# Second layer's weight operands made during the first layer through four buffers and stored to DRAM

## The chip, the cores and the metric

One core of a Trainium2 chip. The time is device microseconds of one execution of the whole kernel; where several runs are named, it is their median. TensorE multiplies, ACT (ScalarE), DVE (VectorE) and POOL (GpSimd) do everything elementwise, SP (SyncE) issues nearly all DMAs. Each engine works through its own queue in order.

## The reference

Float32 all through. Attention in chunks of 32 queries over a window of keys plus 8 memory keys, for 4 x 8 heads of 768 x 64; its output, laid out as x of 3072 tokens x 512, goes through two feed-forward layers:

```python
# per chunk of 32 queries: mem_k, mem_v and 16 positions to the left, 8 to the right
a = softmax(q_c @ [mem_k, k_ctx].T / 8);  attn_c = a @ [mem_v, v_ctx]
x = attn, heads side by side                     # 3072 x 512
h = x @ moe_w_in;  x = (h * cos(h)) @ moe_w_out  # layer 1, d_ff 2048
h = max(max(x @ w1, x @ w2), x @ w3)             # layer 2, d_ff 768
out = h @ moe2_w_out
```

## The kernel before, in words

**Split operands.** TensorE's operands have the type fp32r, so each float32 operand is kept as two tiles, high part and remainder, and each product is three matmuls (`PASSES`). The weights arrive as 64-bit words; making an operand out of a raw tile `[128, 512, 2]` takes: the load (`w_load`, L163), the exponent part (`w_top`, ACT or POOL, L174), the mantissa merged into it (`w_bits`, DVE, L185), and the split, a copy on ACT and a subtraction on DVE or POOL (`w_split` L199 for layer 1 and w_out of layer 2, `q_split` L500 for w1 to w3).

**Layer 1.** The tokens are 8 blocks j = 0 to 7 of 384, d_ff is 16 chunks f of 128. A slot is one (j, f): `p1` (L384) makes h with 12 matmuls, `chain` (L399) makes g = h cos h on ACT, DVE, ACT, DVE, ACT, POOL (L421 to L431), `p2` (L435) multiplies g with w_out two slots later, 12 more matmuls into four accumulators. There are 128 slots; the order is blocks 0 to 5, then blocks 6 and 7 in halves, and `turn`, slot 104, is the first of block 7. Between p1 and p2 a slot can hold a piece of the attention of the next block (tables `FIRST` to `STEADY`: S scores, E exponentials, N normalizing, T transposes, V values). Block results go to DRAM (`x2d`).

**Layer 2.** Four pairs p of blocks. For each pair nine quads q, each a pair of 128-column chunks of one of w1, w2, w3, as seven products of 6 matmuls in place of eight (`PRODUCTS`, sums and differences of weights and of x), so 42 matmuls of 384 columns a quad and 378 a pair. The results are copied out of PSUM (`snap`, L705, ACT), added (L708) and maximized. Then 108 matmuls with w_out of layer 2 (L780). A quad reads four operand tiles from DRAM (`wd`), three of 512 KB and one of 256 KB, fetched three quads ahead (`q_fetch`, L515).

**Preparation.** `wd` must be made first, out of w1 to w3: eight steps for each of nine quads (`q_steps`, L522: tops, bits, four POOL sums, four splits, then `q_store`, L509, which stores four tiles), and two steps for each of six chunks of w_out (`o_steps`, L555), which stay on chip. `Prep` (L563) loads and steps through this from slot `turn` on, in the 24 last slots of layer 1 up to three steps a slot (`fill`, L879), and goes on inside the quads of pair 0 (L981 to L984). It uses the 32 buffers of pool `wp`, which hold all weights of layer 1; a buffer comes free when block 7 has used its weight. `live` counts them.

**Order.** A scheduler orders each engine's instructions when the kernel is built: by program order, but an instruction whose inputs are expected earlier may go ahead. `keep` puts an instruction behind the one traced just before it on its engine. Instructions of the preparation are kept on ACT, DVE and POOL; loads and stores on SP are not.

Of the kernel before, what the change touches and what calls it, by code (L numbers as in the profile page):

```python
# [9 lines left out]
F32 = mybir.dt.float32  # L10
# [60 lines left out]

NW, NTOP = 32, 2
RATE = 2
STEPS = 3

# [5 lines left out]
def attn_moe_kernel(ctx, tc, qT, kT, vw, w_in, w_out, w3, w2o, out):  # L83
# [22 lines left out]
    ps_acc = ctx.enter_context(tc.tile_pool(name="ps_acc", bufs=1, space=PSUM))  # L106
    ps_h = ctx.enter_context(tc.tile_pool(name="ps_h", bufs=2, space=PSUM))
    ps_a = ctx.enter_context(tc.tile_pool(name="ps_a", bufs=2, space=PSUM))
    att_cm = tc.tile_pool(name="att", bufs=2)
    t2 = att_cm.__enter__()  # L110
    tmp = {}
# [51 lines left out]
    def w_load(key):  # L163

        kind, i = key
        src = SRC[kind][i] if kind != "b" else w3[i[0], i[1]]
        t = wp.tile([128, 512, 2], I32, tag="w", name="raw")
        live[0] += 1
        SP.dma_start(out=t.rearrange("p c t -> p (c t)").bitcast(U16)[:, :2047], in_=src.bitcast(U16)[:, 1:])
        wst[key] = t  # L170

# [13 lines left out]
    def w_bits(key):  # L185

        z = o = wst[key][:, :, 0]
        if key[0] == "out" and key[1] < PLAIN:
            i, odd = divmod(key[1], 2)
            if not odd:  # L190
                plain[i] = (wp if i < PLAIN // 2 - 1 else tmp["pool"]).tile([128, 2, 512], I32, tag="w", name="wt")
                live[0] += i < PLAIN // 2 - 1
            o = plain[i][:, odd, :]
            live[0] -= 1
            DST[key[0]][key[1]] = o.bitcast(F32)
        keep(DVE.scalar_tensor_tensor(o, z, 13, top[key], op0=ALU.logical_shift_right, op1=ALU.bitwise_or))  # L196
        wst[key] = o.bitcast(F32)
# [258 lines left out]
    hB, xs, x2, wq, post = {}, {}, {}, {}, {}  # L456
    bank = [0]
    wd = [[dp.tile([128, 1024 if i < 3 else 512], F32, name=f"wd{q}_{i}") for i in range(4)] for q in range(NQ)]

    def w_tile(shape, name, dtype=F32R):  # L460
        live[0] += 1
        assert live[0] <= NW
        return wp.tile(shape, dtype, tag="w", name=name)
# [36 lines left out]
    def q_split(q, i, eng):  # L500
        ev, od = q_parts(q)
        src = (ev[0], ev[1], od[0], od[1][:, :256])[i]
        n = 512 if i < 3 else 256
        w = w_tile([128, 2, n], "wq")
        keep(ACT.activation(out=w[:, 0, :], in_=src, func=AF.Copy))
        keep(eng.tensor_tensor(w[:, 1, :], src, w[:, 0, :].bitcast(F32), op=ALU.subtract))
        wq["new", q, i] = w

    def q_store(q):  # L509
        for i in range(4):  # L510
            w = wq.pop(("new", q, i))
            SP.dma_start(out=wd[q][i], in_=w.rearrange("p a c -> p (a c)").bitcast(F32))
            live[0] -= 1

    def q_fetch(p, q):  # L515
        for i in range(4):
# [5 lines left out]
    def q_steps(q):  # L522

        a, b = q_pair(q)

        def bits(k):
            raw = wst[k]
            w_bits(k)
            wst[k] = raw
        L, R = slice(0, 256), slice(256, 512)  # L530

        def s_31():
            ev, od = q_parts(q)
            q_sub(POOL, od[0][:, L], ev[0][:, L], ev[1][:, L])
            q_sub(POOL, ev[1][:, L], ev[1][:, L], ev[1][:, R], ALU.add)

        def s_2():
            ev, od = q_parts(q)
            q_split(q, 0, DVE)
            q_sub(POOL, od[0][:, R], ev[1][:, L], ev[0][:, L])  # L540

        def s_4():
            ev, od = q_parts(q)
            q_sub(POOL, od[1][:, L], ev[0][:, R], od[0][:, R])
            q_split(q, 1, DVE)

        def end():
            q_split(q, 3, POOL)
            live[0] -= 2
            wst.pop(a), wst.pop(b), qs.pop(q)  # L550
            q_store(q)
        return [lambda: w_top(a, ACT), lambda: (w_top(b, ACT), bits(a)), lambda: bits(b), s_31, s_2, s_4,
                lambda: q_split(q, 2, DVE), end]

    def o_steps(f):  # L555
        key = ("bo", f)

        def go():
            w_top(key, ACT)
            w_bits(key)  # L560
        return [go, lambda: w_split(key, DVE)]

    class Prep:  # L563


        def __init__(self):
            self.nl = self.n = 0
            self.loads = [("q", q) for q in range(NQ)] + [("o", f) for f in range(FB)]
            self.steps = [(i, fn) for i, (kind, n) in enumerate(self.loads)
                          for fn in (q_steps(n) if kind == "q" else o_steps(n))]  # L570

        def load(self):
            while self.nl < len(self.loads):
                ahead = self.nl - (self.steps[self.n][0] if self.n < len(self.steps) else self.nl)
                if ahead >= (2 if self.loads[self.nl][0] == "q" else 3):
                    return
                kind, n = self.loads[self.nl]
                if live[0] + (8 if kind == "q" else 3) > NW:
                    return
                if kind == "q":  # L580
                    q_load(n)
                else:
                    w_load(("bo", n))
                self.nl += 1

        def go(self, n=1):
            for _ in range(n):
                if self.n < len(self.steps) and self.steps[self.n][0] < self.nl - (self.nl < len(self.loads)):
                    if self.steps[self.n][0] < NQ and live[0] + 1 > NW:
                        return  # L590
                    self.steps[self.n][1]()
                    self.n += 1

        def made(self):
            return self.steps[self.n][0] if self.n < len(self.steps) else len(self.loads)


    def x_load(p, which=(0, 1)):
# [243 lines left out]
                w_split(("out", self.ns), POOL if self.ns % 2 else DVE)  # L842
                self.ns += 1

    tmp_open("wt", 1)
    dec = Decode(keysA, lambda n: POOL if n < 6 or n % 2 else ACT, lambda n: POOL if n % 2 else DVE)
    for c in LOADS.split():
        if c[0] == "q":
# [16 lines left out]
    def slot(s):  # L865
# [13 lines left out]
        def fill(where):  # L879
            if s < 2:  # L880
                if where == "z":
                    dec.split_in(ready)
                    dec.bits()
                    dec.load()
                return
            if s >= turn:
                if where == "z":
                    prep.load()
                    for fn in early.get(s - total, ()):
                        fn()  # L890
                    if s < total - 6:
                        prep.go(1)
                elif where in ("a0", "d0"):
                    prep.go(1)
                return
            if where == "a0":
                dec.split_in(ready)
            elif where == "a1":
                dec.split_out(parts)
            elif where == "d0":  # L900
                dec.bits(1)
            elif where == "z":
                dec.bits()
                dec.exp(dec.nb + 2)
                dec.load()
# [31 lines left out]
                a_load_v(d + 2)  # L937
        do2()

    prep = Prep()  # L940
    early = {}
    ops0 = {}

# [1 line left out]
        x_sum(0)  # L945
        ops0.update(x_ops(0))

    early[-9] = [lambda: x_load(0)]
    early[-7] = [begin0, lambda: ops0["b11"]()]
    early[-6] = [lambda: ops0["t1"]()]  # L950
    early[-5] = [lambda: ops0["t2"]()]
    early[-4] = [lambda: ops0["t4"]()]
    early[-3] = [lambda: ops0["b22"](), lambda: ops0["t3"](), lambda: q_fetch(0, 0)]
    early[-2] = [lambda: q_fetch(0, 1)]
    early[-1] = [lambda: ops0["rest"]()]
    for s in range(total):
        if s == turn:
            tmp_close()
            att_cm.__exit__(None, None, None)
            tmp_open("ph2", 2)  # L960
            done[0] = True
            prep.load()
        slot(s)
        if s < PINNED:
            hold()
    hold(False)
    rest = [slots[i] for i in range(n2[0], total)]
    for p in range(NP):
        for q in range(NQ):
            for n in quad(p, q):  # L970
                if p == 0 and q == 0 and n < 3:
                    while len(rest) > (2, 1, 0)[n]:
                        p2(*rest.pop(0))
                if n == 0:
                    if p == 0 and q == 0:
                        q_fetch(0, 2)
                    nxt = divmod(p * NQ + q + AHEAD, NQ)
                    if nxt[0] < NP and (nxt[0] == p or parts[2 * p + 2] == 1 or nxt[1] == 0):
                        assert p or nxt[0] or prep.made() > nxt[1], (q, prep.made())
                        q_fetch(*nxt)  # L980
                if p == 0:  # L981
                    if n % 2 == 0:
                        prep.load()
                    prep.go(STEPS if n == 6 else 1)  # L984
                if q == NQ - 2 and n == 0 and p + 1 < NP:
                    x_load(p + 1, (0,))
                if q == NQ - 1 and n == 0 and p + 1 < NP:
                    x_load(p + 1, (1,))
# [82 lines left out]
```

## Time and profile before

| | us |
|---|---|
| median of 3 runs | 1059.85 (1059.73 to 1060.57) |
| profiled execution | 1060.66 |
| its span | 1058.9 |
| TensorE busy, weight loads busy | 1007.4, 959.0 |
| DVE, ACT, POOL busy | 572.5, 501.4, 405.4 |

The mean granted TensorE clock is 0.982 of full speed. The busy time of TensorE is modelled from pipelined matmuls, so 95% busy is not 95% of its peak; idle time of an engine that others don't wait for costs nothing. In the rows below PE is TensorE, PEld its weight loads, L705 is line 705 of the kernel, and "x <- y" in the name of an instruction is what it writes and reads.

### The profile page before, as it was taken

How to read it: one execution, taken by the hardware profiler on the slowest of the kernel's cores; microseconds unless marked ns; L12 is line 12 of the kernel's file. 1: busy time of each engine (PE TensorE's matmuls, PEld its weight loads, DVE VectorE, ACT ScalarE, POOL GpSimd, SP SyncE). 2: the span in 40 equal slices, each digit the busy share in tenths (PEclk: the TensorE clock that was granted, in tenths of full speed). 3: DMA queues.
4: the chain of work that ended last, by engine and by line, in shares of the span. 5: the costliest groups of instructions: out<-in, count | busy, mean ns of one | idle time of the engine just before them, and what ended most of it. 6: DMA issues, size and time to landing. Idle time of an engine off the chain costs nothing.

```text
span 1058.9 us, 17399 instructions
## 1 busy us (share of the span) xinstructions
PE 1007.4 (95%) x6732; PEld 959.0 (91%) x6733; DVE 572.5 (54%) x1002; ACT 501.4 (47%) x930; POOL 405.4 (38%) x370
## 2 busy tenths in 40 slices
PE   8799999999999999999999997676999999999998
PEld 5679999999999999999999997666989989999997
DVE  7876566554554545454444676565544464464451
ACT  5578555545555554545544565444333333333331
POOL 4575453333333333333223555462423342433330
PEclk9999999999999999999999998987999999999999
DMA  9951111111111211110112676999339718746601
GB/s 293 361 235 46 53 61 61 67 39 39 67 38 38 68 38 41 65 38 29 48 55 74 244 263 218 397 413 380 132 139 348 257 52 345 231 181 229 247 1 60
DMA packets 55906, 158.67 MB, mean 150 GB/s; under 512 B 6288, under 2 KB 11664, under 8 KB 55824
## 3 DMA queue, kind: packets, MB, share of 16 engines
q1 hardware_dynamic: 55680, 157.43, 41.7%
q8 instruction: 53, 0.87, 0.3%
q14 instruction: 29, 0.24, 0.1%
q10 hardware_dynamic: 144, 0.13, 0.0%
HBM read 126.86 MB, written 30.67 MB: 149 GB/s over the span
## 4 chain that ended last, share of the span: by engine, by line
PE 80%; DMA 10%; DVE 3%; ACT 2%; issue 2%; POOL 2%; SPq 1%; POOLq 0%; ACTq 0%; DVEq 0%
PE h L382 22%; PE hb L684 21%; PE acc L382 21%; PE hb L780 9%; DMA wq<-wd 3%; PE s L242 3%; DMA raw<-in_w_out_dram 2%; PE s L296 2%; PE s L280 2%; DMA k<-in_kT_dram 1%; DMA raw<-in_w_in_dram 1%; DMA raw<-in_w_dram 1%; DMA wd<-wq 1%; DMA raw<-in_w2o_dram 1%; DVE raw L196 0%
## 5 line engine op out<-in xcount | busy, mean ns | idle before, releaser
L382 PE MATMUL h<-x,w 128*128 128x384 f32 x1536 | 291.4, 337 | 5.2 <-DVE g L413 3.8
L382 PEld LDWEIGHTS h<-x,w 128*128 128x128 f32 x1536 | 266.8, 188 | 9.9 <-DVE g L413 4.7
L382 PE MATMUL acc<-g,w 128*128 128x384 f32 x1440 | 273.7, 338 | 1.8 <-POOL g L431 0.7
L382 PEld LDWEIGHTS acc<-g,w 128*128 128x128 f32 x1440 | 252.1, 189 | 3.5 <-DVE x L450 1.2
L431 POOL TENSOR_TENSOR g<-ki,g 128x384 fp32r<-128x384 f32 x112 | 115.0, 1027 | 265.9 <-ACT g L430 213.3
L684 PE MATMUL hb<-x,wq 128*128 128x384 f32 x864 | 157.3, 336 | 7.1 <-DMA wq<-wd 7.1
L684 PEld LDWEIGHTS hb<-x,wq 128*128 128x128 f32 x864 | 151.6, 189 | 7.6 <-DVE ki L424 7.4
L684 PE MATMUL hb<-xo,wq 128*128 128x384 f32 x648 | 125.8, 349 | 26.3 <-ACT a L705 26.3
L684 PEld LDWEIGHTS hb<-xo,wq 128*128 128x128 f32 x648 | 119.5, 198 | 27.5 <-ACT a L705 27.5
L423 DVE SCALAR_TENSOR_TENSOR ki<-h,ki 128x384 f32<-128x384 f32 x112 | 62.1, 555 | 121.2 <-ACT ki L421 121.2
L426 ACT ACTIVATE ki<-ki,pio 128x384 f32<-128x384 f32 x112 | 68.9, 616 | 90.8 <-DVE ki L424 90.8
L780 PE MATMUL hb<-w,g 128*128 128x512 f32 x432 | 98.7, 389 | 0.0
L428 DVE TENSOR_TENSOR ki<-h,ki 128x384 f32<-128x384 f32 x112 | 62.4, 557 | 64.2 <-ACT ki L426 64.0
L780 PEld LDWEIGHTS hb<-w,g 128*128 128x128 f32 x432 | 81.0, 188 | 16.7
L421 ACT ACTIVATE ki<-h 128x384 int32<-128x384 f32 x112 | 54.5, 487 | 71.8 <-PE h L382 69.9
L708 POOL TENSOR_TENSOR p<-p,p 128x384 f32<-128x384 f32 x36 | 36.8, 1023 | 133.4 <-ACT p L705 133.4
L430 ACT ACTIVATE g<-ki 128x384 fp32r<-128x384 f32 x112 | 58.6, 524 | 60.2 <-DVE ki L428 59.8
L708 DVE TENSOR_TENSOR a<-a,hb 128x384 f32<-128x384 f32 x36 | 19.9, 553 | 79.9 <-PE hb L684 79.9
L424 DVE TENSOR_SCALAR ki<-ki 128x384 f32<-128x384 f32 x112 | 53.5, 477 | 2.7
L708 POOL TENSOR_TENSOR p<-p,u 128x384 f32<-128x384 f32 x36 | 37.3, 1036 | 41.4 <-ACT u L705 39.9
L196 DVE SCALAR_TENSOR_TENSOR raw<-raw,top 128x512 int32<-128x512 int32 x48 | 41.1, 862 | 20.9 <-ACT top L179 20.7
L272 POOL TENSOR_TENSOR sm<-sm,rs 128x768 f32<-128x768 f32 x21 | 31.2, 1491 | 54.8 <-DVE rs L271 48.9
(115 smaller groups left out, 1108.8 us busy)
## 6 DMA issues: line engine op xcount, KB each, us to landing
wq<-wd SPq DMA_DIRECT2D x108, 512.0 KB, 7.1
wd<-wq SPq DMA_DIRECT2D x27, 512.0 KB, 3.8
v<-in_vw_dram SPq DMA_DIRECT2D x24, 384.0 KB, 4.5
wq<-wd SPq DMA_DIRECT2D x36, 256.0 KB, 7.7
raw<-in_w_dram SPq DMA_DIRECT2D x18, 511.8 KB, 6.0
raw<-in_w_in_dram SPq DMA_DIRECT2D x16, 511.8 KB, 10.2
raw<-in_w_out_dram SPq DMA_DIRECT2D x16, 511.8 KB, 10.2
k<-in_kT_dram SPq DMA_DIRECT2D x24, 320.0 KB, 4.4
```

The source lines that it names most:

```text
L196: keep(DVE.scalar_tensor_tensor(o, z, 13, top[key], op0=ALU.logical_shift_right, op1=ALU.bitwise_or))
L382: PE.matmul(o, lhsT=w[a][:, sl], rhs=x[b], start=first and n == 0, stop=last and n == 2)
L421: ACT.activation(out=ki, in_=h, func=AF.Copy, scale=INV2PI, bias=0.25)
L423: DVE.scalar_tensor_tensor(c, h, INV2PI, ki, op0=ALU.mult, op1=ALU.subtract)
L424: DVE.tensor_scalar(c, c, -0.75, 0.25, op0=ALU.max, op1=ALU.min)
L426: ACT.activation(out=c, in_=c, func=AF.Sin, scale=2 * math.pi, bias=pio2)
L428: DVE.tensor_tensor(c, h, c, op=ALU.mult)
L430: ACT.activation(out=g[:, 0, :], in_=c, func=AF.Copy)
L431: POOL.tensor_tensor(g[:, 1, :], c, g[:, 0, :].bitcast(F32), op=ALU.subtract)
L684: keep(PE.matmul(o, lhsT=w[:, a, 256 * half + 128 * c:256 * half + 128 * c + 128], rhs=x[c][:, b, :], start=first and n == 0, stop=n == 5, ...
L708: keep(eng.tensor_tensor(o, a, b, op=op))
L780: keep(PE.matmul(o, lhsT=g[:, i, 128 * m:128 * m + 128], rhs=w[k], start=(f == 0 and n == 0), stop=(f == FB - 1 and n == 2)))
```

## The change

All operands of layer 2 are made by slot 101, from slot 31 on: at the end of each slot's `chain` the list `prep` is brought up to int((s - 30) x 1.4) of its 99 steps. The list has one step more than before for each load (nine for a quad, three for a chunk of w_out), so a load comes one step before its first use. Raw tiles and operands of the preparation share four buffers of 4 KB a partition in a new pool `pre`; each operand is stored as soon as it is split, and that frees its buffer. The operands of w_out are stored too (`wod`), and fetched in quads 2 to 4 of pair 0, two a quad (`o_fetch`). Nothing is prepared from slot 102 on. `x_load(0)` moves one slot earlier, the fetches of quads 0, 1 and 2 move to slots total-9, total-3 and total-2. The one buffer of pool `wt` is taken from `pre` instead, and the scratch of the DMA rings shrinks to 1024 bytes.

```diff
-STEPS = 3
+PREP0, PREPS = 30, 1.4
...
+    pre = ctx.enter_context(tc.tile_pool(name="pre", bufs=4))
...
     def w_load(key):
...
-        t = wp.tile([128, 512, 2], I32, tag="w", name="raw")
-        live[0] += 1
+        if kind[0] == "b":
+            t = pre.tile([128, 512, 2], I32, tag="p", name="raw")
+        else:
+            t = wp.tile([128, 512, 2], I32, tag="w", name="raw")
+            live[0] += 1
...
     def q_split(q, i, eng):
...
-        w = w_tile([128, 2, n], "wq")
+        store(src, n, eng, wd[q][i])
+
+    def store(src, n, eng, dst):
+        w = pre.tile([128, 2, n], F32R, tag="p", name="wq")
         keep(ACT.activation(out=w[:, 0, :], in_=src, func=AF.Copy))
         keep(eng.tensor_tensor(w[:, 1, :], src, w[:, 0, :].bitcast(F32), op=ALU.subtract))
-        wq["new", q, i] = w
-
-    def q_store(q):
-        for i in range(4):
-            w = wq.pop(("new", q, i))
-            SP.dma_start(out=wd[q][i], in_=w.rearrange("p a c -> p (a c)").bitcast(F32))
-            live[0] -= 1
+        SP.dma_start(out=dst, in_=w.rearrange("p a c -> p (a c)").bitcast(F32))
...
     def q_steps(q):
...
-        return [lambda: w_top(a, ACT), lambda: (w_top(b, ACT), bits(a)), lambda: bits(b), s_31, s_2, s_4,
+        return [lambda: q_load(q), lambda: w_top(a, ACT), lambda: (w_top(b, ACT), bits(a)), lambda: bits(b), s_31, s_2, s_4,
                 lambda: q_split(q, 2, DVE), end]
...
     def o_steps(f):
...
-        return [go, lambda: w_split(key, DVE)]
-
-    class Prep:
...
+        return [lambda: w_load(key), go, lambda: store(wst.pop(key), 512, DVE, wod[f])]
+
+    prep = [fn for q in range(NQ) for fn in q_steps(q)] + [fn for f in range(FB) for fn in o_steps(f)]
+    prep_n = [0]
+
+    def prep_go(upto):
+        while prep_n[0] < min(upto, len(prep)):
+            prep[prep_n[0]]()
+            prep_n[0] += 1
+
+    def o_fetch(f):
+        w = w_tile([128, 2, 512], "wo")
+        SP.dma_start(out=w.rearrange("p a c -> p (a c)").bitcast(F32), in_=wod[f])
+        wB_out[f] = (w[:, 0, :], w[:, 1, :])
...
         def fill(where):
...
             if s >= turn:
                 if where == "z":
-                    prep.load()
                     for fn in early.get(s - total, ()):
                         fn()
-                    if s < total - 6:
-                        prep.go(1)
-                elif where in ("a0", "d0"):
-                    prep.go(1)
                 return
+            if where == "z":
+                prep_go(int((s - PREP0) * PREPS))
...
-    early[-9] = [lambda: x_load(0)]
+    early[-10] = [lambda: x_load(0)]
...
-    early[-3] = [lambda: ops0["b22"](), lambda: ops0["t3"](), lambda: q_fetch(0, 0)]
-    early[-2] = [lambda: q_fetch(0, 1)]
+    early[-9] = [lambda: q_fetch(0, 0)]
+    early[-3] = [lambda: ops0["b22"](), lambda: ops0["t3"](), lambda: q_fetch(0, 1)]
+    early[-2] = [lambda: q_fetch(0, 2)]
...
                 if n == 0:
-                    if p == 0 and q == 0:
-                        q_fetch(0, 2)
+                    if p == 0 and 1 < q < 5:
+                        o_fetch(2 * q - 4)
+                        o_fetch(2 * q - 3)
...
-                if p == 0:
-                    if n % 2 == 0:
-                        prep.load()
-                    prep.go(STEPS if n == 6 else 1)
...
-    nc = bacc.Bacc("TRN2", target_bir_lowering=False, num_devices=1)
+    nc = bacc.Bacc("TRN2", target_bir_lowering=False, num_devices=1, dynamic_dma_scratch_size=1024)
```

## Rows read from the trace of the kernel before

**Rows 1.** The page's 40 slices, in tenths: TensorE busy, granted clock:
```profile
PE   8799999999999999999999997676999999999998
...
PEclk9999999999999999999999998987999999999999
```

**Rows 2.** Stretches: length; busy PE, PEld, DVE, ACT, POOL; clock, DMA share, GB/s:
```profile
108.00:150.00 42.00, 40.12 (x296) 38.18 (x295) 26.46 (x47) 24.80 (x42) 21.12 (x17) 1.00 0.18 62
...
230.00:530.00 300.00, 300.00 (x2319) 294.31 (x2318) 151.18 (x288) 155.19 (x254) 95.79 (x85) 1.00 0.14 46
...
574.00:626.00 52.00, 52.00 (x301) 51.68 (x299) 34.06 (x55) 31.34 (x61) 30.09 (x31) 1.00 0.63 226
...
644.50:760.60 116.10, 82.75 (x416) 81.50 (x416) 63.94 (x98) 50.14 (x97) 50.28 (x49) 0.84 0.90 344
```

**Rows 3.** Chain of waits: start, length, what; pair 1's products:
```profile
785.12 65.54 PE hb L684 x378
```

**Rows 4.** Waits of TensorE, 600 to 780 us: total, times, longest:
```profile
PE hb L684 <- ACT a L705: 26.3, 4, 9.4
PE hb L684 <- DMA wq<-wd: 7.1, 1, 7.1
PE acc L382 <- ACT x L448: 0.5, 1, 0.5
PE acc L382 <- DVE x L450: 0.4, 1, 0.4
```

**Rows 5.** Timeline of TensorE: start, length, what, idle before it:
```profile
721.62 4.92 PE L684 MATMUL hb<-xo,wq 128*128 128x384 f32 x18 [9.43 <-ACT a L705]
```

**Rows 6.** Waits of ACT for loads, 640 to 765 us:
```profile
ACT top L179 <- DMA raw<-in_w_dram: 12.5, 4, 9.7
...
ACT top L179 <- DMA raw<-in_w2o_dram: 9.7, 2, 7.3
```

**Rows 7.** Groups, 560 to 760.6 us: count, busy us, mean ns, idle before:
```profile
L486 POOL TENSOR_TENSOR raw<-raw 128x256 f32<-128x256 f32 x36 | 33.4, 928 | 20.1 <-DVE raw L196 18.4
...
L506 DVE TENSOR_TENSOR wq<-raw,wq 128x512 fp32r<-128x512 f32 x27 | 26.1, 969 | 19.9 <-ACT wq L505 19.8
...
L179 ACT ACTIVATE top<-raw 128x512 f16<-128x512 bf16 x24 | 18.4, 782 | 22.2 <-DMA raw<-in_w_dram 12.5 <-DMA raw<-in_w2o_dram 9.7
...
L505 ACT ACTIVATE wq<-raw 128x512 fp32r<-128x512 f32 x27 | 17.7, 667 | 16.0 <-POOL raw L486 9.5 <-DMA wd<-wq 4.9 <-DMA wq<-wd 1.6
...
L196 DVE SCALAR_TENSOR_TENSOR raw<-raw,top 128x512 int32<-128x512 int32 x24 | 17.4, 733 | 20.7 <-ACT top L179 20.7
```

**Rows 8.** DMA of 785 to 850 us, beside pair 1's products:
```profile
DMA packets 5910, 18.43 MB, mean 283 GB/s; under 512 B 656, under 2 KB 656, under 8 KB 5904
```

**Rows 9.** Timeline, a plain slot of block 3:
```profile
294.87 1.01 POOL L431 TENSOR_TENSOR g<-ki,g 128x384 fp32r<-128x384 f32 x1 [3.57 <-PE acc L382]
...
300.02 2.24 PE L382 MATMUL acc<-g,w 128*128 128x384 f32 x12
```

**Rows 10.** Timeline, a slot with an exponential; its table loads, 190 to 530 us:
```profile
311.12 0.56 DVE L428 TENSOR_TENSOR ki<-h,ki 128x384 f32<-128x384 f32 x1 [0.57 <-ACT ki L426]
...
314.11 2.24 PE L382 MATMUL h<-x,w 128*128 128x384 f32 x12
...
L264 ACT ACT_TABLE_LOAD x13 | 16.7, 1283 | 0.2
```

**Rows 11.** Timeline of block 1, a slot with an exponential and a split:
```profile
121.98 0.62 PE L382 MATMUL h<-x,w 128*128 128x384 f32 x2 [1.10 <-DVE ki L428]
```

**Rows 12.** Timeline: DVE's clamp alone, and beside POOL's L486:
```profile
301.40 0.36 DVE L424 TENSOR_SCALAR ki<-ki 128x384 f32<-128x384 f32 x1
...
593.62 4.22 POOL L486 TENSOR_TENSOR raw<-raw 128x256 f32<-128x256 f32 x4
...
594.15 1.02 DVE L424 TENSOR_SCALAR ki<-ki 128x384 f32<-128x384 f32 x1
```

**Rows 13.** DMA issues, 544 to 620 us: count, KB each, us to landing:
```profile
raw<-in_w_dram SPq DMA_DIRECT2D x10, 511.8 KB, 4.5
```

More of the change, by code (lines that the diff above doesn't have):

```diff
@@ L190, in w_bits @@
             if not odd:
-                plain[i] = (wp if i < PLAIN // 2 - 1 else tmp["pool"]).tile([128, 2, 512], I32, tag="w", name="wt")
+                plain[i] = (wp if i < PLAIN // 2 - 1 else pre).tile([128, 2, 512], I32, tag="w" if i < PLAIN // 2 - 1 else "p", name="wt")
                 live[0] += i < PLAIN // 2 - 1
@@ L458, in attn_moe_kernel @@
     wd = [[dp.tile([128, 1024 if i < 3 else 512], F32, name=f"wd{q}_{i}") for i in range(4)] for q in range(NQ)]
+    wod = [dp.tile([128, 1024], F32, name=f"wod{f}") for f in range(FB)]
     def w_tile(shape, name, dtype=F32R):
@@ L548, in end @@
             q_split(q, 3, POOL)
-            live[0] -= 2
             wst.pop(a), wst.pop(b), qs.pop(q)
-            q_store(q)
-        return [lambda: w_top(a, ACT), lambda: (w_top(b, ACT), bits(a)), lambda: bits(b), s_31, s_2, s_4,
+        return [lambda: q_load(q), lambda: w_top(a, ACT), lambda: (w_top(b, ACT), bits(a)), lambda: bits(b), s_31, s_2, s_4,
                 lambda: q_split(q, 2, DVE), end]
@@ L560, in go @@
             w_bits(key)
-        return [go, lambda: w_split(key, DVE)]
-    class Prep:
[L566 to L595, printed above, removed]
+        return [lambda: w_load(key), go, lambda: store(wst.pop(key), 512, DVE, wod[f])]
[9 more added lines that the diff above has]
+        wB_out[f] = (w[:, 0, :], w[:, 1, :])
     def x_load(p, which=(0, 1)):
@@ L843, in split_out @@
                 self.ns += 1
-    tmp_open("wt", 1)
     dec = Decode(keysA, lambda n: POOL if n < 6 or n % 2 else ACT, lambda n: POOL if n % 2 else DVE)
@@ L938, in slot @@
         do2()
-    prep = Prep()
     early = {}
@@ L957, in attn_moe_kernel @@
         if s == turn:
-            tmp_close()
             att_cm.__exit__(None, None, None)
@@ L974, in attn_moe_kernel @@
                 if n == 0:
-                    if p == 0 and q == 0:
-                        q_fetch(0, 2)
+                    if p == 0 and 1 < q < 5:
+                        o_fetch(2 * q - 4)
+                        o_fetch(2 * q - 3)
                     nxt = divmod(p * NQ + q + AHEAD, NQ)
                     if nxt[0] < NP and (nxt[0] == p or parts[2 * p + 2] == 1 or nxt[1] == 0):
-                        assert p or nxt[0] or prep.made() > nxt[1], (q, prep.made())
                         q_fetch(*nxt)
-                if p == 0:
-                    if n % 2 == 0:
-                        prep.load()
-                    prep.go(STEPS if n == 6 else 1)
                 if q == NQ - 2 and n == 0 and p + 1 < NP:
```

## The prediction

> **What bounds the kernel now.** I read the page's 40 slices first [rows 1]. The row PE stands at 9 nearly from end to end, except in slices 25 to 28 (26.5 us each), where it falls to 7676; PEclk dips there too. So TensorE bounds the kernel everywhere but in one hole. The table by stretch says the same in numbers [rows 2]: in 230 to 530 us, steady blocks of layer 1, TensorE is busy 300.00 of 300.00 us while DVE (151.18), ACT (155.19) and POOL (95.79) are half or two thirds idle; in 644.5 to 760.6, where pair 0 of layer 2 runs with the last three steps of layer 1, it is busy only 82.75 of 116.1 us, at a granted clock of 0.84 of its higher level (2.4 GHz).
>
> What pair 0 should cost stands in the chain of waits [rows 3]: pair 1 runs the same 378 matmuls of 384 columns without a gap in 65.54 us, 173.4 ns each. Between 644.5 and 760.6 TensorE runs 36 matmuls of layer 1 and those 378 of pair 0: 414 x 0.1734 = 71.8 us. It takes 116.1, so 44.3 us are lost. TensorE's own waits say where [rows 4]: four of 26.3 us in sum and one of 7.1, together 33.4; the rest, 82.75 - 71.8 = 10.95 us, goes to matmuls that run at a lower granted clock after a wait, as the 18 that take 4.92 us after the longest wait [rows 5], where 18 x 0.1734 are 3.1.
>
> Who holds TensorE there: the first wait ends with the fetch wq<-wd, the other four with "ACT a L705", the copy that empties a PSUM bank. That copy is short; it stands in ACT's order behind instructions of the preparation which wait for a DMA. The waits of 640 to 765 us name them [rows 6]: top (L179) for the raw weights of w1 to w3, 12.5 us with 9.7 the longest, and for those of w_out, 9.7 with 7.3. So the hole is preparation that waits for a whole DMA, with TensorE's evictions queued behind it.
>
> **The change, part by part.** *Removed from 540 to 760 us:* all loads, splits and stores of the preparation. The five large groups [rows 7] are ACT 18.4 + 17.7 = 36.1 us, DVE 26.1 + 17.4 = 43.5 and POOL 33.4; the smaller copies and subtractions of the same steps I estimate from them at 8, 4 and 10 more (nine half-size copies, nine POOL subtractions, and six splits of w_out at the 0.67 and 0.97 us of the large ones): 44, 48 and 43. With it go the waits of [rows 6]. The fetch for (0, 0) is issued in slot total-9 instead of total-3, behind no store of that time, so its 7.1 us go. What is late next? In pair 0 the engines then do what they do in pair 1, and there TensorE has no gap [rows 3]. The DMA traffic is pair 1's 18.43 MB [rows 8] plus the six fetches of wod, 3.1 MB: 21.5 MB in 65.5 us, 329 GB/s, below the 344 GB/s of the stretch in question [rows 2]. Quads 2 to 4, with a double load, need 1.84 + 1.05 = 2.9 MB in 7.28 us, 397 GB/s, but each fetch is issued three quads (21.8 us) ahead. I cost this at nothing; if that cover went, a wait like the 7.1 us would come back. Gain here: 44.3 us. Two short waits near 626 us, 0.5 and 0.4 us [rows 4], where accumulator copies stood behind preparation on ACT and DVE, go as well: 0.9 us.
>
> *Moved into slots 31 to 101* (by the position of the blocks some 190 to 530 us): 99 steps at 1.4 a slot. The 44, 48 and 43 us lie beside 340 us of TensorE at work, 13 to 14% more for each engine: DVE 50 to 64%, ACT 52 to 65%, POOL 32 to 45%. No engine becomes the bound. What can hurt is delay on the path from p1 through chain to p2. In a plain slot [rows 9] a g is done at 294.87 + 1.01 = 295.88 us, and the p2 that reads it, two steps on, starts at 300.02: 4.1 us to spare. A slot gets one or two steps, which put about two instructions of 0.67 to 0.97 us ahead of a link on an engine: it fits. In a slot with an exponential ACT has two table loads ahead of the sine; h is freed by DVE L428 only at 311.12 + 0.56 = 311.68, and the p1 that needs the buffer starts at 314.11 [rows 10]: 2.4 us to spare. Such slots are 13 in 190 to 530 us (13 table loads of L264 [rows 10]).
>
> The trace has two stretches like it. Lower bound, 574 to 626 us: up to three steps a slot, DVE busy 66%, POOL 58%, and TensorE 52.00 of 52.00 [rows 2]; but no attention there, and more buffers for h. Upper bound, 108 to 150 us: attention plus seven weight splits, and TensorE 40.12 of 42.00 [rows 2]; at that rate 340 us would lose 1.88 / 42 x 340 = 15.2 us. The larger of its two waits, 1.10 us [rows 11], falls in a slot with an exponential and an added split. At 1.4 steps a slot 0.4 of the slots get two steps; I let those of the 13 lose as much: 13 x 0.4 x 1.10 = 5.7 us, nearer to the lower end, and keep 0 and 15.2 for the range.
>
> The port that DVE and POOL share is the other way in. Beside a POOL subtraction the clamp of the chain (DVE L424) takes 1.02 us instead of 0.36 [rows 12]. POOL gets 45 more instructions; within 4.1 us of room one of them costs nothing, and if the clamp waits out one of 0.93 us [rows 7] in those 13 x 0.4 slots, that is 4.8 us on top. The Trainium skill, "SBUF — State Buffer", section "SBUF: two separate sides", says that the pair of ports is an exclusive lock and that the loser blocks for the whole instruction. By that rule the 4.8 us are lost and the time is 1025.2 us; the trace agrees on the lock, 1.02 against 0.36, and shows no wait of TensorE from it in 574 to 626.
>
> *Waits added.* Four buffers hold two raw tiles and two operands, so the third operand's ACT copy waits for the first one's store, and the next load for the last subtraction; behind these copies on ACT stand the next link of chain, then p2. ACT's order is written by expected times, so what is left is their error. In 544 to 620 us a raw load lands in 4.5 us [rows 13], against 4.1 us of room: nothing, or a few tenths. On SP the loads for attention, a block ahead of use, and the x2d stores stand behind these DMAs: nothing. The wt buffer moves to another pool, and the smaller DMA scratch serves no queue used here (SP and ACT issue all): nothing.
>
> *Sum* against the profiled execution (1060.66 us, span 1058.9): 1060.66 - 44.3 - 0.9 + 5.7 = 1021.2. It lies 0.81 above the median of the runs, 1059.85, so the forecast is 1020.4 us.
>
> **The rivals.** (a) *The moved work costs more in blocks 2 to 6.* For it: the rate of 108 to 150 us. Against it: 574 to 626 us without a loss. At the upper bound, 15.2 instead of 5.7: 1059.85 - 45.2 + 15.2 = 1029.9 us. With the port's share on the forecast: 1020.4 + 4.8 = 1025.2.
> (b) *Pair 0 stays hungry.* The fetches bunch with wod in quads 2 to 4, and waits like the 7.1 and one of 9.4 us [rows 4] stay, with slow clock in proportion (10.95 / 33.4 = 0.33 us per us of wait): 16.5 x 1.33 = 21.9, time 1020.4 + 21.9 = 1042.3. For it: 397 GB/s wanted there. Against: pair 1 without a gap.
> (c) *Slower: four buffers tie ACT to the DMA.* Each load is issued one step before its first use, no longer up to two pairs ahead, and ACT stands at its head through the landing, with chain behind it. There are 15 such places (nine pairs, six chunks of w_out). If each waits like the longest of [rows 6], 9.7 us, less the 4.1 of room, that is 15 x 5.6 = 84 us, time 1059.85 - 45.2 + 84 = 1098.7. It decides from 45.2 / 15 = 3.0 us net a place, 7.1 us at ACT's head. For it: exactly such waits made the hole. Against: they came with the DMA 90% busy; in 230 to 530 it is 14% [rows 2], and in 574 to 626, at 63%, loads of about that time landed in 4.5 us.
> (d) *It doesn't do what it says*: every operand is fetched from DRAM either way, and nothing in the rows speaks for it.
>
> **How the numbers follow.** Forecast without the port's share (1014 to 1023) 0.53, with it (to 1026) 0.12; (a) beyond that, to 1031, 0.18; (b) 0.09; (c) 0.07, of which 0.04 slower than before; (d) 0.01. The range goes from no loss at all (1059.85 - 45.2 = 1014.7) up through (a) to 1033; what is left out, most of (b) and (c), is under 2 in 10. A measurement of this kernel can tell about 0.2% (2 us) from no change. Faster by more than that: 0.94; within it: 0.02; slower by more: 0.04.
>
> **What would show it.** Right: PE 9 and PEclk 9 all through layer 2; pair 0 in one run of about 65.5 us; no L705 and no wq<-wd among TensorE's waits; layer 1 ending some 4 to 6 us later than 644.5, lost in a few waits of about 1 us in slots with an exponential, on DVE L428 or POOL g L431. Wrong: ACT waiting for raw or wd by several us in 190 to 530 (c), TensorE waiting for wq after layer 1 (b), layer 1 later by 10 us and more (a).

## The result, and the profile after

The kernel after takes 1018.62 us (median of 4 runs, 1017.12 to 1021.01) against 1059.79 of the kernel before beside it: a ratio of 0.9612, 95% interval 0.9592 to 0.9633. Its profiled execution took 1017.12 us, with a span of 1015.3. Lines of the chain and the copies stand four lines further down than before (`chain`'s last product is L435, the copies of the accumulators L452 and L454, the splits L513 and L514), those of layer 2 some twenty further up (products L663, their copies L684).

The page's slices that answer [rows 1], TensorE and granted clock:

```profile
PE   8899999999999999999999999999999999999998
...
PEclk9999999999999999999999999999999999999999
```

The hole of slices 25 to 28 is gone, and the clock stays at its higher level. The stretches, as in [rows 2] (length; busy PE, PEld, DVE, ACT, POOL; clock, DMA share, GB/s); the last is now pair 0 with the last three steps of layer 1:

```profile
190.00:540.00 350.00, 347.75 (x2695) 339.83 (x2694) 218.94 (x386) 211.57 (x359) 152.77 (x142) 1.00 0.40 135
230.00:530.00 300.00, 297.75 (x2301) 291.22 (x2301) 189.90 (x336) 183.19 (x309) 133.66 (x125) 1.00 0.41 138
...
644.50:716.90 72.40, 72.40 (x419) 72.40 (x418) 32.60 (x57) 24.80 (x51) 25.41 (x24) 1.00 0.75 280
```

DVE is at 63% of 230 to 530 us where it was at 50, ACT at 61 (52), POOL at 45 (32). Pair 0 has TensorE busy without a gap. The chain of waits says the same beside [rows 3]:

```profile
654.52 62.40 PE hb L663 x360
716.92 24.52 PE hb L759 x108
741.44 65.54 PE hb L663 x378
```

Of pair 0's 378 products the last 360 run in one piece; the first 18 lie among layer 1's last p2 from 645.00 us on. TensorE's waits of 600 to 780 us, four kinds in [rows 4], are none at all now. Those of layer 1 between 190 and 540 us are new:

```profile
PE acc L386 <- DVE x L454: 1.7, 2, 1.2
PE h L386 <- DVE ki L432: 0.6, 1, 0.6
```

Three waits, 2.25 us in sum: 1.19 at 285.70, 0.49 at 442.23, 0.57 at 526.18. How the first arises is read from the timeline of the three engines (start, length, what, idle before it):

```profile
278.64 2.33 DVE L514 TENSOR_TENSOR wq<-raw,wq 128x512 fp32r<-128x512 f32 x2 [1.15 <-ACT wq L513]
280.89 0.55 DVE L427 SCALAR_TENSOR_TENSOR ki<-h,ki 128x384 f32<-128x384 f32 x1
...
284.05 1.00 POOL L435 TENSOR_TENSOR g<-ki,g 128x384 fp32r<-128x384 f32 x1 [2.60 <-ACT g L434]
...
285.08 0.56 DVE L454 COPY x<-acc 128x384 f32<-128x384 f32 x1 [1.67 <-POOL g L435]
...
285.70 0.79 PE L386 MATMUL acc<-g,w 128*128 128x384 f32 x3 [1.19 <-DVE x L454]
```

Two splits of the preparation follow each other on DVE and hold up the chain's L427; so g comes late on POOL (285.05), and only then is one of the four buffers free that chain and accumulator copies share (pool `tr`). The copy that empties the accumulator waits 1.67 us for it, and the next block's p2 for the copy. The wait at 442.23 ends with the same links; ahead of them stand one split of 1.24 us and a clamp (L428) of 0.76 us beside one of POOL's sums. In 190 to 540 us ACT waits for no load; these take from issue to landing (DMA issues, as in [rows 13]):

```profile
raw<-in_w_dram SPq DMA_DIRECT2D x16, 511.8 KB, 4.1
```

So the time came from pair 0: its products ended at 760.6 us and end at 716.9, 43.7 us earlier, and the span is 43.6 shorter.

### The profile page after: what moved, and what is told of

Read it like the earlier page. It is cut to its first block, busy times and chain, and to the rows that moved or that the text cites. A ratio compares the mean times of both kernels' runs of the same rounds, so it can differ in the third digit from the quotient of the medians.

```text
span 1015.3 us, 17456 instructions
## 1 busy us (share of the span) xinstructions
PE 998.9 (98%) x6733; PEld 951.4 (94%) x6733; DVE 570.6 (56%) x1002; ACT 498.7 (49%) x930; POOL 403.6 (40%) x370
## 4 chain that ended last, share of the span: by engine, by line
PE 82%; DVE 4%; POOL 3%; issue 3%; ACT 2%; POOLq 0%; ACTq 0%
PE hb L663 26%; PE h L386 21%; PE acc L386 20%; PE hb L759 10%; PE s L246 2%; PE s L300 2%; PE s L284 2%; POOL g L435 1%; POOL raw L491 1%; POOL sm L276 1%; DVE ki L427 0%; DVE raw L200 0%; DVE ki L432 0%; DVE ki L428 0%; POOL sm L264 0%
## 5 line engine op out<-in xcount | busy, mean ns | idle before, releaser
L386 PEld LDWEIGHTS h<-x,w 128*128 128x128 f32 x1536 | 268.1, 189 | 10.9 <-DVE g L417 4.8
L435 POOL TENSOR_TENSOR g<-ki,g 128x384 fp32r<-128x384 f32 x112 | 115.5, 1031 | 246.3 <-ACT g L434 207.1
L663 PE MATMUL hb<-x,wq 128*128 128x384 f32 x864 | 156.1, 334 | 0.0
L663 PEld LDWEIGHTS hb<-x,wq 128*128 128x128 f32 x864 | 150.4, 188 | 0.2
L663 PE MATMUL hb<-xo,wq 128*128 128x384 f32 x648 | 118.1, 334 | 0.0
L663 PEld LDWEIGHTS hb<-xo,wq 128*128 128x128 f32 x648 | 112.8, 188 | 0.0
L427 DVE SCALAR_TENSOR_TENSOR ki<-h,ki 128x384 f32<-128x384 f32 x112 | 61.9, 553 | 82.7 <-ACT ki L425 80.7
L759 PE MATMUL hb<-wo,g 128*128 128x512 f32 x432 | 98.7, 389 | 0.0
L432 DVE TENSOR_TENSOR ki<-h,ki 128x384 f32<-128x384 f32 x112 | 62.3, 556 | 64.6 <-ACT ki L430 64.5
L759 PEld LDWEIGHTS hb<-wo,g 128*128 128x128 f32 x432 | 81.0, 188 | 16.7
L428 DVE TENSOR_SCALAR ki<-ki 128x384 f32<-128x384 f32 x112 | 52.7, 471 | 2.8
L684 ACT ACTIVATE a<-hb 128x384 f32<-128x384 f32 x36 | 17.6, 488 | 74.3 <-PE hb L663 74.3
L276 POOL TENSOR_TENSOR sm<-sm,rs 128x768 f32<-128x768 f32 x21 | 31.3, 1492 | 51.4 <-DVE rs L275 42.6
```

What stands on the lines that cost most here:

```text
L276: POOL.tensor_tensor(m, m, r[:, :, None].to_broadcast([128, H, KU]), op=ALU.mult)
L386: PE.matmul(o, lhsT=w[a][:, sl], rhs=x[b], start=first and n == 0, stop=last and n == 2)
L427: DVE.scalar_tensor_tensor(c, h, INV2PI, ki, op0=ALU.mult, op1=ALU.subtract)
L428: DVE.tensor_scalar(c, c, -0.75, 0.25, op0=ALU.max, op1=ALU.min)
L432: DVE.tensor_tensor(c, h, c, op=ALU.mult)
L435: POOL.tensor_tensor(g[:, 1, :], c, g[:, 0, :].bitcast(F32), op=ALU.subtract)
```

## The experiments

The twelve runs came in three sets, each with the kernel before beside it (1059.57, 1059.81 and 1061.73 us). Runs of one set are compared by their medians; across sets the ratios to before are compared, a thousandth being 1.06 us.

**What the moved work costs in layer 1.** e1_again is the kernel after unaltered.

> The changed kernel unaltered, for a second trace and as the yardstick of the other runs. Its four runs lie between 1017.12 and 1021.01 us, four times the spread of the kernel before. If TensorE's new waits in layer 1 (1.19 + 0.49 + 0.57 us in the first trace, behind evictions of the accumulators and one sine) vary with the arrival of DMAs, this trace shows other waits in 190 to 530 us and their sum follows the time; if the spread comes from the start (the first 60 us, where loads bind), the waits in 190 to 530 us are the same again and the difference lies before 108 us.

1018.75 us, ratio 0.9609 (0.9597 to 0.9622). The second case holds: TensorE loses 2.29 us in 190 to 540 against 2.25; the span, 1.8 us longer than the first time, differs at the start (in the first 60 us TensorE is busy 50.36 against 52.55).

e2_noprep leaves all preparation out:

```diff
-    prep = [fn for q in range(NQ) for fn in q_steps(q)] + ...
+    cz = pre.tile([128, 1024], F32, tag="p", name="cz")
...
+    def put(dst, n):
+        return lambda: SP.dma_start(out=dst, in_=cz[:, :2 * n])
...
+    prep = [fn for q in range(NQ) for fn in [none] * 5 + [put(wd[q][i], ...) for i in range(4)]]
+    prep += [fn for f in range(FB) for fn in [none, none, put(wod[f], 512)]]
```

> Leaves out all preparation of layer 2's weights, its loads and its work on ACT, DVE and POOL; a constant tile is stored in place of each operand, at the same steps. It shows what the moved work costs layer 1. Theory: only TensorE's few new waits, so 2 to 4 us below the changed kernel (first trace: 2.25 us). Rival: the moved work costs the 5.7 us of the prediction or more and something else gave back a part, so 6 us and more below it. Rival: it is hidden wholly, within 1 us.

1016.31 us (0.9590, 0.9574 to 0.9605). The sum of the same stretch, 190 to 540 us, first in this run:

```profile
sum 350.00, PE 350.00 PEld 342.76 DVE 174.56 ACT 179.24 POOL 110.78; mean PE 350.00 PEld 342.76 DVE 174.56 ACT 179.24 POOL 110.78
```

and in e1_again:

```profile
sum 350.00, PE 347.71 PEld 339.67 DVE 219.06 ACT 211.26 POOL 153.86; mean PE 347.71 PEld 339.67 DVE 219.06 ACT 211.26 POOL 153.86
```

The preparation adds 45 us to DVE's busy time, 32 to ACT's and 43 to POOL's there and costs TensorE 2.3; by the medians 2.4, as the theory had it (the two intervals overlap, so the traces are the firmer ground). That is what the moved work gives back of the gain; the stores, which this run keeps, cost TensorE nothing in this stretch.

e3_edge keeps the steps out of the first two slots of each block, e12_gentle lets at most one into the last three and starts earlier:

```diff
-PREP0, PREPS = 30, 1.4
+PREP0, PREPS = 24, 1.56      # e3_edge; e12_gentle: 24, 1.28
-                prep_go(int((s - PREP0) * PREPS))
+                prep_c[0] += s >= PREP0 and f > 1                         # e3_edge
+                prep_go(int(prep_c[0] * PREPS))
...
+                prep_go(upto if f < 13 else min(upto, prep_n[0] + 1))     # e12_gentle
```

> No step of the preparation in the first two slots of a block (f = 0 and 1, in which the accumulators of the block before are emptied), steps in all other slots from 24 on at 1.56 a slot, so that it ends by slot 100. If TensorE's new waits come where the evictions stand behind a split on DVE, the two waits for x (1.19 and 0.49 us) go and the time falls by 1.5 to 2 us. Rival: waits depend on where steps and exponentials meet, so the sum of the waits stays at 2 us or more and the time is the same within 1 us.

> The kernel after with its steps from slot 25 on at 1.28 a slot, and at most one step in the slots f = 13 to 15, so that the copies of the accumulators at the end of a block don't meet two splits. Theory (the 2.3 us that remain come from two steps in one slot, above all at the end of a block): 1 to 2 us of them go, 1016.5 to 1018 us. Rival (as in e3_edge, other meetings take their place): 1018 to 1021 us.

e3_edge: 1020.83 us (0.9635, 0.9621 to 0.9649), 2.1 over e1_again; e12_gentle: 1019.88 (0.9612, 0.9596 to 0.9627), level with it. The waits of TensorE in 190 to 540 us, of e3_edge:

```profile
PE h L386 <- DVE ki L432: 2.6, 3, 1.2
PE acc L386 <- DVE x L454: 1.4, 1, 1.4
```

and of e12_gentle:

```profile
PE acc L386 <- DVE x L454: 1.5, 2, 1.1
PE h L386 <- DVE ki L432: 1.4, 2, 1.2
```

My theory fell twice: kept away from one meeting place, the steps meet the chain at another. No version tried here beats the kernel after by an amount that can be told.

**Buffers and rate.** e7_bufs3 takes one of the four buffers away; e8_dense does the same steps at 2.62 a slot in slots 31 to 68; e4_late does so in slots 90 to 127, right ahead of pair 0.

```diff
-    pre = ctx.enter_context(tc.tile_pool(name="pre", bufs=4))
+    pre = ctx.enter_context(tc.tile_pool(name="pre", bufs=3))    # e7_bufs3
-PREP0, PREPS = 30, 1.4
+PREP0, PREPS = 30, 2.62      # e8_dense; e4_late: 89, 2.62, also from slot turn on
```

> The kernel after, with three buffers in the pool of the preparation in place of four: with two raw tiles held, each operand's ACT copy waits until the store before it has landed. Theory (in blocks 2 to 6 steps are far enough apart that such a wait ends before ACT reaches the copy): TensorE loses 0 to 5 us more than in the kernel after, 1017 to 1024 us. Rival (c) of the prediction (a wait for the DMA at ACT's head passes on to chain and p2): nine quads with three such waits of 2 us or more each, at least 10 us, 1029 us or more.

1020.26 us (0.9620, 0.9592 to 0.9649): no difference that can be told, as the theory had it. ACT now waits 5.7 us in all for raw (seven times, 1.8 at most), and the room in the slots swallows it: TensorE loses 2.7 us in 190 to 540. The number of buffers is not what counts at this rate.

> The same preparation through the same four buffers at 2.62 steps a slot in slots 90 to 127, the end of layer 1, still all done before pair 0. If the gain comes from taking the preparation out of pair 0, it stays: pair 0 in one run of about 65.5 us, and the price is only a denser layer 1, 0 to 8 us above the changed kernel. Rival: four buffers can't keep this rate (a load of 4.2 us, stores of 2.7 us, twice a quad's preparation in series), ACT waits for DMAs and the fetches of the last quads wait for their stores: 15 us and more above it.

1055.93 us (0.9961, 0.9945 to 0.9976): 37 us over e1_again, nearly all of the gain. The theory fell, the rival's size held. In e4_late's timeline, ACT and TensorE where layer 1 ends:

```profile
685.15 0.77 ACT L183 ACTIVATE top<-raw 128x512 f16<-128x512 bf16 x1 [11.10 <-DMA raw<-in_w2o_dram]
...
688.12 0.69 PE L663 MATMUL hb<-x,wq 128*128 128x384 f32 x1 [10.07 <-ACT x L602]
690.01 1.97 PE L663 MATMUL hb<-x,wq 128*128 128x384 f32 x5 [1.20 <-POOL x L603]
```

ACT stands at its head for 11.10 us for one load of w_out. SP issues that load only at 677.57, 3.5 us into the wait, behind a store that waited for its split and four loads of pair 0's operands; among the fetches it takes 7.5 us to land. Behind ACT's wait stands L602, which splits x for layer 2, and TensorE waits 10.07. This is rival (c)'s mechanism at full price, in the one place where the room ahead of it is gone. It is the largest of TensorE's waits, 28.2 us in all from 480 us on, of which 9.5 come before 640; the granted clock is 0.72 in 663 to 700. The run carries the dense rate as well; e8_dense has the rate alone.

> The kernel after, with the same steps at 2.62 a slot in place of 1.4, in slots 31 to 68: the rate of the run e4_late, but far from pair 0. Theory A (what cost 37 us there was the meeting with the fetches of pair 0 and its start, not the rate): the stretch of 480 to 600 us of that run, 24 slots at this rate ahead of the fetches, lost 5.4 us; over 38 slots that is 8 to 9 us, less the 2.3 us that the kernel after loses: 1022 to 1028 us, with no wait of ACT for a load over 2 us. Theory B (four buffers can't follow this rate, wherever it is): ACT waits for loads by several us again and passes it on, 18 us and more, 1036 us or more.

1038.02 us (0.9785, 0.9752 to 0.9817), 19 us over the kernel after: theory A fell. B held in size, but no single wait of ACT for a load is several us long: it waits for the raw weights of w1 to w3 nine times, 2.3 us at most and 11.8 in all. TensorE's waits are for the chain (L432, 10.9 us of 180 to 400). In e8_dense's timeline of ACT, DVE, POOL and TensorE ahead of one of 2.85 us:

```profile
264.05 4.19 POOL L491 TENSOR_TENSOR raw<-raw 128x256 f32<-128x256 f32 x4
...
266.32 0.67 ACT L513 ACTIVATE wq<-raw 128x512 fp32r<-128x512 f32 x1 [2.57 <-POOL raw L491]
...
267.02 0.74 DVE L514 TENSOR_TENSOR wq<-raw,wq 128x512 fp32r<-128x512 f32 x1 [1.91 <-ACT wq L513]
267.69 0.77 DVE L428 TENSOR_SCALAR ki<-ki 128x384 f32<-128x384 f32 x1
...
269.75 3.85 PE L386 MATMUL h<-x,w 128*128 128x384 f32 x12 [2.85 <-DVE ki L432]
```

Steps that meet in a slot put four sums in a row on POOL; the split's copy stands at ACT's head for them, the split at DVE's head for the copy, and the chain's L428 behind the split. e11_dense_nosum takes the sums away:

```diff
     def q_sub(eng, o, a, b, op=ALU.subtract):
-        keep(eng.tensor_tensor(o, a, b, op=op))
+        pass
...
-        src = (ev[0], ev[1], od[0], od[1][:, :256])[i]
+        src = (ev[0], ev[1], ev[0], ev[1][:, :256])[i]
```

> e8_dense without POOL's four sums a quad (the operands of w1 to w3 are split from the unsummed halves, so the products are not those of the reference); loads, copies, splits and stores are the same in number and size, through the same four buffers. Theory (what cost e8_dense 19 us is ACT standing at the split's copy until POOL has made up to four sums in a row, with DVE and the chain behind it): most of the 19 us go, 1018 to 1026 us. Rival (four buffers and the loads set the limit): the loss stays, 1032 us or more.

1028.09 us (0.9687, 0.9663 to 0.9711). By the ratios 8 of 19 us are left: about half of the loss is POOL's sums, short of "most". The run takes away both ACT's waits for them and the port that they share with DVE, but the clamp's mean falls only from 467 to 425 ns in 180 to 400 us, which speaks for the waits as the larger part. TensorE's largest wait for L432 falls from 3.2 us to 1.7. What the other half is (the rows show copies and splits in a row ahead of the chain, and 13.7 us of short waits of ACT for raw) I did not separate. More than four buffers were not tried.

**What the hole of pair 0 was made of.** Traffic alone, engine work alone and both together are put into pair 0 of the kernel after (lines of e6, e9 and e10 stand one to eight further down):

```diff
...
+                if p == 0 and q < 6:                  # e5_traffic, e10_both
+                    if n in (0, 2):
+                        keep(SP.dma_start(out=t, in_=wd[(q + n) % NQ][0]))
+                    elif n in (1, 3, 5):
+                        keep(SP.dma_start(out=dd[q][n // 2], in_=cz))
+                if p == 0 and q < 6:                  # e6_compute; e9_match, e10_both: 1
+                    for _ in range(3 if n == 6 else 1):
+                        fake[fake_n[0] % 8]()         # q_steps(0) again, stores left out
+                        fake_n[0] += 1
```

> The kernel after, with DMA traffic added in quads 0 to 5 of pair 0 that nobody waits for: two more loads of 512 KB and three stores of a constant 512 KB tile a quad, 15.7 MB in all, on SP's queue. All of the computation is done. Theory (the hole of the kernel before was ACT waiting at its head for loads, with the copies out of PSUM queued behind; the traffic by itself was not what TensorE waited for): pair 0 has 37 MB to move in some 65 us; if the fetches wq<-wd still come in their order three quads ahead, TensorE waits 0 to 3 us, 1019 to 1022 us. Rival (traffic is the root: the transfers of preparation and fetches together did not fit): at the 400 GB/s or so that the DMA moved at its densest in the runs so far, 37 MB take 92 us, so TensorE waits some 25 us for wq<-wd, and with the lower clock after such waits the time is 1040 to 1055 us.

1025.83 us (0.9672, 0.9641 to 0.9703), 7 us over after. TensorE's waits of 640 to 740 us in e5_traffic:

```profile
PE hb L663 <- DMA wq<-wd: 5.6, 2, 4.0
```

Neither prediction: 15.7 MB more do reach the fetches, which now take 9.7 us to land, but cost 7 us, not 25 and more.

> The kernel after, with the engine work of 54 steps of preparation (6.75 of the nine quads) repeated in quads 0 to 5 of pair 0 on raw tiles that are on chip already, without loads and stores: ACT +27 us, DVE +29.5 us, POOL +32 us in the 44 us of these quads. What it adds feeds nothing, and the computation is that of the kernel after. Theory (ACT's wait for loads made the hole, not the load on the engines): DVE would be asked for 49 us of work in 44, so pair 0 may stretch by up to 6 us, with short waits of 1 us or so for L684; 1019 to 1026 us. Rival (the engines were too full in pair 0 before, whatever the loads did): waits for the copies out of PSUM of 15 us and more, with the lower clock after them, 1035 to 1055 us.

1042.58 us (0.9820, 0.9787 to 0.9853), 22 over after: theory fell, the rival's time held, with 13.8 us of waits for the copies out of PSUM where it said 15 and more. So loads are not the only way into such a hole. ACT's wait is this one (waits of ACT, 640 to 750 us):

```profile
ACT wq L514 <- POOL raw L492: 26.0, 14, 5.1
```

Without any load ACT still stands at its head, for POOL's sums, and the copies out of PSUM behind it. But this run asks for more in less time than the kernel before had in pair 0 (28 sums against 16).

> As e6_compute, but with one step a product in quads 0 to 5 of pair 0 (42 steps in place of 54, with 14 tops as in pair 0 of the kernel before); no loads, no stores, and what it adds feeds nothing. Theory (ACT's wait at its head for POOL's sums costs something by itself, and the waits for loads the rest of the 41 us): with fewer steps side by side less than half of e6_compute's 24 us, 1022 to 1031 us. Rival A (the engine work makes most of the hole): 20 us and more, 1039 us or more. Rival B (without loads this amount of work is free): 1018 to 1021 us.

1031.93 us (0.9722, 0.9707 to 0.9737), 12 us over after by the ratios, with somewhat fewer tops than the kernel before had there (12 against 14) and more sums (20 against 16). It lies 0.9 us above the theory's range; A and B both fell. TensorE's waits of 640 to 735 us in e9_match, against 33.4 us in [rows 4]:

```profile
PE hb L671 <- ACT a L692: 8.0, 2, 5.4
PE hb L671 <- ACT p L692: 2.0, 2, 1.1
```

> e9_match and the added traffic of e5_traffic together in pair 0, neither waiting for the other. Theory (the rest of the hole is engines standing at their head for a DMA that they need, which is not in this run): the two losses add up, that is 7 us over e9_match, well short of the kernel before: 1028 to 1040 us. Rival (work and traffic do it without any wait of one for the other): 1050 to 1060 us.

1032.31 us (0.9717, 0.9693 to 0.9741). TensorE's waits of 640 to 740 us in e10_both:

```profile
PE hb L671 <- ACT a L692: 8.0, 2, 5.4
PE hb L671 <- ACT p L692: 1.9, 2, 1.0
```

The same as without the traffic, so the two don't add up; I take it that a pair that is 12 us longer has room for 15.7 MB more, which is not tested. The time lies in the theory's range, but not by its sum. The rival fell: work and traffic that don't wait for each other cost some 12 us, where the change gains 41.

These 12 us are no share of the 41, though. In the kernel before, ACT waited much less for POOL's sums than the 13.6 us of e9_match, and more for DMAs (waits of ACT, 640 to 765 us, beside [rows 6]):

```profile
ACT wq L505 <- DMA wd<-wq: 4.9, 2, 4.0
ACT wq L505 <- POOL raw L486: 3.5, 3, 2.6
```

What stands ahead of TensorE's waits is seen in the timelines of ACT and TensorE before:

```profile
685.36 0.77 ACT L179 ACTIVATE top<-raw 128x512 f16<-128x512 bf16 x1 [9.67 <-DMA raw<-in_w_dram]
...
687.78 4.79 PE L684 MATMUL hb<-xo,wq 128*128 128x384 f32 x18 [8.61 <-ACT a L705]
...
720.46 0.77 ACT L179 ACTIVATE top<-raw 128x512 f16<-128x512 bf16 x1 [7.33 <-DMA raw<-in_w2o_dram]
```

The wait of 8.61 us ends behind ACT's 9.67 for a load (one more top stands between), and the one of 9.43 [rows 5] right behind its 7.33: 18.0 of the 26.3 us. A third, 5.16 us, has two short waits for loads (1.84 and 0.52) and some 3 us of ACT's own work ahead of it; the fourth, 3.07 us, follows a wait of 2.19 us for DVE's L196. With the 7.1 us for the fetch, 25.1 of the 33.4 us of waits [rows 4] end behind a DMA that the trace names. How the rest divides between loads and engine work is open: no run has the links alone.

## Why the prediction came out right

Forecast 1020.4 us, measured 1018.62; faster, within the likeliest case's own range.

- *Pair 0's price, and what goes.* 44.3 us: right. From pair 0's first product (645.00) to the last (716.8) it now takes the 71.8 us worked out from [rows 3]. The clock is at its higher level throughout, so the 10.95 us of slow matmuls went with the waits.
- *What held TensorE.* Right for the greater part. Two of the four waits, 18.0 of 26.3 us, end behind ACT's waits for loads, and e4_late has the same link. Put too wide was "instructions of the preparation which wait for a DMA": the wait of 3.07 us stands behind DVE, and e9_match, with a like amount of work and no load, still loses 12 us, by ACT's waits for POOL's sums. The change takes both away, so the sum didn't suffer.
- *"I cost this at nothing": the fetches.* Right, with less cover than it looked. In the kernel after no product waits for wq, while the fetches of 512 KB take 7.6 us to land and the DMA moves 372 GB/s between 663 and 700 us; with e5_traffic they reach 9.7 us and TensorE waits.
- *Near 626 us.* The two waits of 0.9 us are gone.
- *The moved work: the term that was mis-sized.* "13 x 0.4 x 1.10 = 5.7 us" is 2.25 in the trace and 2.4 in e2_noprep. The bounds, 0 and 15.2, held it. The place was wrong too: no slot of 190 to 540 us loses by two table loads and a step; the waits came at the end of a block, through the buffers that chain and accumulator copies share, and once beside attention work in block 6 (526.18, behind a step's L200 on DVE). The work itself was sized well: by their durations its instructions take 43.9 us on ACT, 52.5 on DVE and 42.6 on POOL in the kernel after, forecast 44, 48 and 43. Layer 1 reaches pair 0 0.5 us later than before, not 4 to 6. The 3.4 us between 5.7 and 2.25 are most of the 4.1 between the sum and the profiled execution (1021.2 and 1017.12); layer 1 also began 0.4 us earlier (the wait of [rows 11] ends at 121.59), and 0.3 stay unassigned. That the medians lie only 1.8 us apart is luck in part: the profiled execution after is 1.5 us below its median, where the one before was 0.81 above.
- *The port.* The clamp's mean rose from 458 to 489 ns in 180 to 540 us, and a split on DVE took 1.02 us against 0.97 in [rows 7]. The 4.8 us by the rule of the Trainium skill ("SBUF — State Buffer", "SBUF: two separate sides") did not come: all that TensorE lost there is 2.25 us. The lock is seen in the durations and is mostly covered by the room in the slots; in the wait at 442.23 a clamp of 0.76 us is one of the links.
- *Waits added by four buffers.* "Nothing, or a few tenths": right at 1.4 steps a slot, where even three buffers do. Rival (c) lost on its condition, not on its mechanism: no head of ACT waited 7.1 us, and where one did, in e4_late, TensorE paid 10.07 for 11.10.
- *Rivals (a), (b) and (d)* did not come; e8_dense shows (a)'s direction, at nearly twice the rate.

## What to carry to other kernels

When preparation starves a bound engine, price the hole by the same stage run without it (here pair 1) and look for stretches where the other engines are half idle; moved there thinly, 32 to 45 us of busy time an engine cost 2.4. Density and distance decide: the same steps at 2.62 a slot cost 21 us, and right ahead of the stage that reads them 40. An in-order engine that waits at its head for anything, a load or another engine's sum, passes the wait on to all that stands behind it, so place what waits where nothing urgent follows.

## What the runs showed of the hardware that was not expected

The DMA kept 400 GB/s and more for tens of us where it was asked for it (e5_traffic moved 401 to 415 GB/s in 660 to 720 us, with 512 KB landing in 9.7 us instead of 7.6), and TensorE, which needed a part of it, lost 7 us. TensorE's granted clock stayed at 1.00 in 190 to 540 us of e3_edge, with four waits of 0.4 to 1.4 us far apart. In e8_dense the 12 matmuls behind the wait of 2.85 us ran at a mean of 0.55 (269.7 to 273.4 us) and took 3.85 us, where 12 others take 2.24. In e4_late four waits within 25 us, 17.8 us in sum, brought the mean of 663 to 700 us down to 0.72.
